# The first z loaded once and turned two neighbouring tiles at a time, with matmuls of zeros ahead and two first squares on ScalarE

## The chip, the core and the metric

The kernel runs on one NeuronCore of one Trainium2 chip. TensorE multiplies and transposes into PSUM, VectorE (DVE) and ScalarE (ACT) work on SBUF and PSUM, GpSimd (POOL) fills constants and issues indirect transfers, and SyncE (SP) issues most of the direct ones; ACT issues a few at the start. The metric is the device time of one execution in microseconds. The span of the profile is a little shorter than that time.

## The reference

Two blocks follow each other. The first is a gated attention over 8 batches of 2496 rows, the second sends each row to one of 8 experts by a hash of its token.

```python
scores = (1 / S) * z @ z.T              # z: (8, 2496, 64)
attn   = maximum(scores, 0) ** 2
x      = (u * (attn @ v)).reshape(B * S, 256)
for e in range(8):                      # rows with token_ids * 2654435761 % 8 == e
    out[mask] = maximum(x[mask] @ w1[e], 0) @ w2[e]     # 256 -> 1024 -> 256
```

Everything is in float32.

## The kernel before

A batch has T = 20 tiles of 128 rows; the last one, tile TM = 19, holds only R = 64 rows. Rows lie in the tiles so that partition p of tiles 0 to 18 holds 19 neighbouring rows of the batch; the 64 last rows are the short tile. Twenty tiles make NG = 5 groups of G = 4 tiles, and a batch is worked through group by group: the group's 512 columns are the queries, and all 20 tiles are the keys.

The order of all instructions is written out by hand (a manual schedule: each engine runs its instructions as the program lists them). It runs like this:

- **Loads.** `load_z(0)`, `load_v(0)`, `load_u(0, 0)` and `load_tokens()` are called first (lines 442 to 445). z of batch 0 is wanted with its 64 columns twice, side by side, so that one transpose of a [128 x 128] tile gives z transposed in partitions 0 to 63 and once more in partitions 64 to 127. So `load_z(0)` (lines 121 to 125) reads z from memory twice, once on SP's queue and once on ACT's, into a tile `[P, T, 2, K]`; its pieces in SBUF are 64 numbers, 256 bytes, long. `tiles_io` (lines 100 to 112) issues one transfer for tiles 0 to 18 and, with `twice=True`, two for the short tile, into partitions 0 to 63 and 64 to 127. v, u and the later batches' z follow on SP's queue; the token ids are on ACT's.
- **Turning.** `turn_z(0, g)` (lines 155 to 158) transposes the four tiles of a group on TensorE into one PSUM tile `z_ps`, and ScalarE copies it whole into `zT`. Later batches are turned on VectorE (line 153).
- **Scores.** `scores(b, g)` multiplies, for every tile t, the turned tile t with the turned group (line 181). Even t use partitions 0 to 63 of `zT`, odd t partitions 64 to 127; such a pair of 64-row matmuls runs on TensorE at the same time. The relu goes to ScalarE or VectorE in turn (lines 185 to 188) and the tile is noted in `to_square`.
- **Squares.** `square(n)` takes the n oldest tiles from that list. In batch 0 it works on VectorE (line 202), in the others on ScalarE (line 200). Ahead of the first group it is called with EARLY = 2 (line 474), after all 20 relus of the group are issued.
- **Attention.** `attend` (line 256) multiplies the squared tile with v into two accumulators, tile by tile; the squares of tiles two ahead, pieces of the routing (`places`, between lines 297 and 416, on VectorE mostly) and the indirect writes are put between. `gate` (line 265) multiplies with u, and `place_x` (line 433) writes the rows to `x_rows` in expert order.
- **Experts.** After the attention, blocks of 256 rows are read back and go through the two expert matmuls (lines 566 and 579), and the result is written by an indirect transfer (line 582). The first expert matmuls wait for the first rows read back.

PSUM buffers with the tag `mm` form one ring of six: the five `z_ps` tiles and the score tiles share it in the order of use. `zn`, the loaded z, has one buffer; the load of batch 1 into it waits until batch 0 is turned. `zero` is a [128 x 256] tile of zeros, filled by GpSimd (lines 281 and 282), from which SP later clears `x_rows` (line 288). `odd` is a [64 x 256] scratch tile for the last short group of a batch (line 236).

Of the kernel before, what the change touches and what calls it, by code (L numbers as in the profile page):

```python
# [10 lines left out]
F32 = mybir.dt.float32  # L11
# [13 lines left out]
def kernel(  # L25
# [10 lines left out]
    nc = tc.nc  # L36

    B, S, D = u.shape
    K = z.shape[-1]
    N = B * S  # L40
    E, _, F = moe_w1.shape
# [3 lines left out]
    P = 128  # L45
    TM = S // P
    SM = TM * P
    R = S - SM
    T = TM + 1
    assert R == 64 and K == 64  # L50
    G = 4
# [13 lines left out]
    def pool(name, bufs, **kw):  # L65
        return ctx.enter_context(tc.tile_pool(name=name, bufs=bufs, **kw))

    const = pool("const", 1)
    mm_ps = pool("mm_ps", 6, space=bass.MemoryType.PSUM)
    acc_ps = pool("acc_ps", 2, space=bass.MemoryType.PSUM)  # L70
    npool = pool("npool", 1)
# [12 lines left out]


    short = const.tile([P, T, R], F32)
    nc.gpsimd.memset(short[R:P, TM, :], 0.0)
    odd = const.tile([R, D], F32)
    ident = const.tile([P, P], F32)
    make_identity(nc, ident[:])  # L90

    def width(t):
        return P if t < TM else R

    def group(g):
        return range(g * G, min(T, g * G + G))

    def tiles_io(dram, b, tiles, sb, store, eng, twice=False):  # L100

        rows = dram[ds(b * S, S), :]
        whole = [t for t in tiles if t < TM]
        pairs = []
        if whole:
            n = len(whole)
            pairs.append((rows[0:SM, :].rearrange("(p t) d -> p t d", t=TM)[:, ds(whole[0], n), :], sb[:, 0:n, :]))
        if TM in tiles:
            for i in range(2 if twice else 1):
                pairs.append((rows[SM:S, :], sb[ds(i * R, R), len(whole), :]))  # L110
        for d, s in pairs:
            eng.dma_start(out=d if store else s, in_=s if store else d)

    uf, vf, zf = (x.rearrange("b s d -> (b s) d") for x in (u, v, z))
    zn, zT, v_sb, u_sb, x_sb, made, mirror, to_square, to_turn, gated = {}, {}, {}, {}, {}, {}, {}, [], [], []
# [3 lines left out]

    def load_z(b):  # L120
        if b == 0:
            zn[b] = npool.tile([P, T, 2, K], F32, name="zn")
            for i in range(2):
                tiles_io(zf, b, range(T), zn[b][:, :, i, :], False, nc.scalar if i else nc.sync, twice=True)
            return
        zn[b] = npool.tile([P, T, NQ, Q], F32, name="zn")
        rows = zf[ds(b * S, S), :]
        for q in range(NQ):
            cols = ts(q % 2, Q)
            o = zn[b][ts(q, Q)]  # L130
            for t, m in ((slice(0, TM), rows[0:SM, cols].rearrange("(j i t) k -> i t j k", i=Q, t=TM)),
                         (TM, rows[SM:S, cols].rearrange("(j i) k -> i j k", i=Q))):
                if t == TM:
                    for h in range(2):
                        nc.sync.dma_start(o[:, TM, ds(h * R // Q, R // Q), :], m)
                else:
                    nc.sync.dma_start(o[:, t], m)

    def load_v(b):
        v_sb[b] = vpool.tile([P, T, D], F32, name="v_sb")  # L140
        for g in range(NG):
            tiles_io(vf, b, group(g), v_sb[b][:, g * G:, :], False, nc.sync, twice=True)
# [5 lines left out]
    def turn_z(b, g):  # L148
        if g == 0:
            zT[b] = zpool.tile([P, T * P], F32, name="zT")  # L150
        o = zT[b][:, ts(g, G * P)]
        if b:
            nc.vector.transpose(o, zn[b][:, ts(g, G)].rearrange("p t j k -> p (t j k)"))
            return
        ps = mm_ps.tile([P, G * P], F32, name="z_ps", tag="mm")
        for i, t in enumerate(group(g)):
            nc.tensor.transpose(ps[:, ts(i, P)], zn[b][:, t].rearrange("p h k -> p (h k)"), ident[:])  # L157
        nc.scalar.copy(o, ps[:])

    def whole(g):  # L160

        return range(G if g < NG - 1 else G - 1)
# [5 lines left out]
    def mirrored(b):  # L168
        return b > 0

    def fresh(b, g):

        return range(g * G if mirrored(b) else 0, T)

    def scores(b, g):

        n = sum(width(t) for t in group(g))
        for t in fresh(b, g):
            h = ds(t % 2 * K, K)
            ps = mm_ps.tile([P, G * P], F32, name="s_ps", tag="mm")  # L180
            nc.tensor.matmul(ps[:, 0:n], zT[b][h, ts(t, P)], zT[b][h, ds(g * G * P, n)], start=True, stop=True)  # L181
            if t % G == 0:
                made[b, g, t // G] = apool.tile([P, G, G * P], F32, name="a", tag="a")
            a = made[b, g, t // G][:, t % G, 0:n]
            if t % 4 == 3 or t % 4 == 1 and not mirrored(b):
                nc.vector.tensor_scalar_max(a, ps[:, 0:n], 0.0)  # L186
            else:
                nc.scalar.activation(a, ps[:, 0:n], AF.Relu)  # L188
            to_square.append((b, g, t))

    def square(n):
        for b, g, t in to_square[:n]:
            a = made[b, g, t // G][:, t % G, :]
            m = len(whole(g)) * P
            pairs = [(a[:, 0:m], a[:, 0:m])]
            if m < G * P:
                pairs.append((short[0:width(t), t, :], a[0:width(t), ds(m, R)]))
            for o, x in pairs:
                if mirrored(b):
                    nc.scalar.square(o, x)  # L200
                else:
                    nc.vector.tensor_mul(o, x, x)  # L202
            if mirrored(b) and t // G > g and (t % G == G - 1):
                to_turn.extend((b, g, t // G, r, c) for r in range(NQ) for c in range(NQ))
        del to_square[:n]
# [72 lines left out]
    token = const.tile([P, B, T], I32)  # L278

    tok = const.tile([P, B, T, 2], I32)  # L280
    zero = const.tile([P, D], F32)
    nc.gpsimd.memset(zero[:], 0.0)
    CLEAR = T // 2
    assert NS % CLEAR == 0

# [144 lines left out]
    def place_x():  # L430
# [5 lines left out]
        tc.declare_no_dep(st.ins, group="x", reason="each token has its own slot")  # L436
        tc.add_to_no_dep_group("x", st.ins)

    order = tc.manual_schedule()
    order.__enter__()  # L440

    load_z(0)
    load_v(0)
    load_u(0, 0)
    load_tokens()
    for g in range(NG):
        turn_z(0, g)
# [3 lines left out]
    EARLY = 2  # L451
# [3 lines left out]
    i = 0  # L455
# [15 lines left out]

    mirror_pool = ExitStack()
    scores(0, 0)
    square(EARLY)
    for n, (b, g) in enumerate(groups):
        if n + 1 < len(groups):
            load_u(*groups[n + 1])
        if g == 0 and b + 1 < B:
            load_z(b + 1)
            load_v(b + 1)  # L480
# [5 lines left out]
        for k in range(2):  # L486
            for t in range(EARLY):
                attend(b, g, t, acc, [2 * k, 2 * k + 1])
            square(2)
            turn_scores(2)  # L490
            between()
        for t in range(EARLY, TM - LATE):
            if g == NG - 1 and b + 1 < B and t % 2 == 0 and t // 2 <= NG:
                turn_z(b + 1, t // 2 - 1)
            attend(b, g, t, acc, range(G))
            if t % G == G - 1 and (b, t // G, g) in mirror and g < NG - 1:
                mirrors.append(mirror.pop((b, t // G, g)))
            square(2)
            turn_scores(2 + (t % 3 == 0))
            between()  # L500
# [6 lines left out]
        if n + 1 < len(groups):  # L507

            while len({k[:3] for k in to_turn}) + len(fresh(*groups[n + 1])) // G > NG + (g + 1 < NG):
                turn_scores(1)  # L510
            scores(*groups[n + 1])
# [140 lines left out]
```

## Time and profile before

| what | value |
|---|---|
| median of three runs | 2717.02 us (2716.9 to 2718.02) |
| the profiled execution's own time | 2718.32 us |
| its span | 2716.4 us |
| TensorE, matmuls | 2681.2 us busy, 99% of the span |
| VectorE, ScalarE, GpSimd busy | 1190.3, 576.2, 478.7 us |
| granted TensorE clock, mean | 0.997 |
| first matmul (a transpose, line 157) starts at | 9.46 us |
| first attention matmul (line 256) starts at | 24.17 us |
| first expert matmul (line 566) waits for rows read back | 15.3 us |

The profile is read as follows. The page gives each engine's busy time, then the groups of instructions by line with the mean duration of one, and the idle time before them with what ended it. The chain of waits goes back from the last instruction to what released each step; its window on the first 60 us shows the start of the kernel. The timeline lists instructions in order of time. The table by windows gives each engine's busy time in a stretch, the granted clock and the transfer rate. The table of transfers gives the median time from issue to landing. All times are counted from the start of the span.

### The profile page before, as it was taken

Reading aid. Unit: us, or ns where it says so; the run is one execution under the profiler, and the core shown is the slowest. Engines: PE = TensorE matmul, PEld = TensorE weight load, DVE = VectorE, ACT = ScalarE, POOL = GpSimd, SP = SyncE. Lnnn points to the kernel's source line nnn. Section 1 sums busy time; section 2 is a strip of 40 time slices with the busy share of each in tenths; the row PEclk is TensorE's granted clock in tenths of the full one; section 3 lists DMA queues with packets and bytes.
Section 4 is the critical chain, followed back from the end, with each engine's and each line's share of the span. In section 5 each row is a group of like instructions: output and inputs, shape, how many; then the busy total and the mean of one; then the engine's idle time right before and its main releaser. Section 6 shows DMA issues by size and latency. Waiting matters only on the chain.

```text
span 2716.4 us, 32950 instructions
## 1 busy us (share of the span) xinstructions
PE 2681.2 (99%) x12650; PEld 2250.2 (83%) x12650; DVE 1190.3 (44%) x1875; ACT 576.2 (21%) x1151; POOL 478.7 (18%) x500
## 2 busy tenths in 40 slices
PE   8999999999999999999999979999999999999998
PEld 6777887888888887887878868888888888888887
DVE  5655956848838838758659411111111111111111
ACT  2013214214222233123132101111111111111111
POOL 0221222122212221222101111111111111111111
PEclk9999999999999999999999989999999999999999
DMA  9612113013103121031101077777777777777773
GB/s 283 212 31 73 32 31 88 16 32 88 31 23 82 31 50 60 26 89 32 32 15 31 23 191 189 188 188 188 194 190 193 191 189 191 190 189 188 189 186 104
DMA packets 334256, 308.84 MB, mean 114 GB/s; under 512 B 186732, under 2 KB 293117, under 8 KB 334096
## 3 DMA queue, kind: packets, MB, share of 16 engines
q1 hardware_dynamic: 309424, 264.78, 38.5%
q0 software_dynamic: 20496, 41.10, 5.0%
q8 instruction: 102, 1.67, 0.3%
q10 hardware_dynamic: 4176, 0.82, 0.2%
q14 instruction: 58, 0.48, 0.1%
HBM read 243.25 MB, written 64.13 MB: 113 GB/s over the span
## 4 chain that ended last, share of the span: by engine, by line
PE 55%; issue 37%; POOL 6%; DMA 2%; POOLq 0%; DVE 0%
PE acc L256 44%; PE s_ps L181 8%; POOL out_dram L582 5%; PE acc L250 1%; DMA out_dram<-o_sb,idx 1%; PE q_ps L231 1%; DMA zn<-in_z_dram 0%; POOLq L582 0%; POOL x_rows L433 0%; PE z_ps L157 0%; DVE upto L350 0%; DVE x_sb L265 0%; DVE a L202 0%; POOLq L647 0%; PE cnt_ps L345 0%
## 5 line engine op out<-in xcount | busy, mean ns | idle before, releaser
L256 PE MATMUL acc<-v_sb,a 128*128 128x256 f32 x3760 | 826.8, 380 | 2.5 <-DVE a L202 1.4
L256 PEld LDWEIGHTS acc<-v_sb,a 128*128 128x128 f32 x3760 | 711.0, 190 | 128.0 <-issue 29.0
L215 DVE STREAM_TRANSPOSE m<-a 32x512 f32<-32x512 f32 (+1 forms) x1120 | 757.2, 676 | 19.5 <-ACT a L200 2.7
L566 PE MATMUL h_ps<-zT,w 128*128 128x256 f32 x2592 | 587.2, 380 | 16.5 <-DMA zT<-x_rows 15.3
L579 PE MATMUL o_ps<-w,hT 128*128 128x256 f32 x2592 | 585.2, 379 | 0.0
L566 PEld LDWEIGHTS h_ps<-zT,w 128*128 128x128 f32 x2592 | 493.6, 191 | 84.6 <-issue 15.7
L579 PEld LDWEIGHTS o_ps<-w,hT 128*128 128x128 f32 x2592 | 492.5, 190 | 66.9
L574 DVE TENSOR_SCALAR hT<-h_ps 128x512 f32<-128x512 f32 x162 | 112.0, 691 | 951.4 <-PE h_ps L566 951.4
L256 PE MATMUL acc<-v_sb,m 128*128 128x256 f32 x2016 | 439.7, 379 | 0.0
L256 PEld LDWEIGHTS acc<-v_sb,m 128*128 128x128 f32 x2016 | 383.1, 190 | 52.0
L188 ACT ACTIVATE a<-s_ps 128x512 f32<-128x512 f32 (+1 forms) x365 | 193.6, 593 | 913.5 <-PE s_ps L181 905.0
L433 POOL DMA_INDIRECT x_rows<-x_sb,slot_i x160 | 157.8, 986 | 1089.8 <-DVE x_sb L265 917.1
L582 POOL DMA_INDIRECT out_dram<-o_sb,idx x162 | 157.5, 972 | 978.8 <-ACT o_sb L581 964.0
L181 PE MATMUL s_ps<-zT 64*128 64x512 f32 (+1 forms) x1040 | 230.4, 586 | 0.0
L186 DVE TENSOR_SCALAR a<-s_ps 128x512 f32<-128x512 f32 (+1 forms) x155 | 106.0, 684 | 283.1 <-PE s_ps L181 282.0
L200 ACT ACTIVATE a<-a 128x512 f32<-128x512 f32 (+1 forms) x420 | 221.5, 623 | 0.0
L581 ACT COPY o_sb<-o_ps 128x256 f32<-128x256 f32 x162 | 60.3, 372 | 743.7 <-PE o_ps L579 743.7
L181 PEld LDWEIGHTS s_ps<-zT 64*128 64x128 f32 x1040 | 116.8, 187 | 89.1 <-issue 61.5
L421 POOL DMA_INDIRECT slot_tokens<-token,addr x160 | 159.3, 996 | 161.2 <-DVE addr L415 110.9
L572 ACT ACTIVATE hT<-h_ps 128x512 f32<-128x512 f32 x162 | 96.7, 597 | 242.1 <-PE h_ps L566 242.1
L265 DVE SCALAR_TENSOR_TENSOR x_sb<-acc,u_sb 128x256 f32<-128x256 f32 x152 | 57.7, 419 | 58.4 <-PE acc L256 57.8
L238 DVE TENSOR_TENSOR odd<-odd,q_ps 64x256 f32<-64x256 f32 x8 | 3.3, 414 | 168.9 <-ACT odd L236 168.9
(67 smaller groups left out, 331.5 us busy)
## 6 DMA issues: line engine op xcount, KB each, us to landing
w<-in_moe_w_dram SPq DMA_DIRECT2D x324, 256.0 KB, 6.7
w<-in_moe_w_dram SPq DMA_DIRECT2D x81, 1024.0 KB, 6.1
x_rows<-zero SPq DMA_DIRECT2D x10, 2176.0 KB, 15.0
zT<-x_rows SPq DMA_DIRECT2D x324, 64.0 KB, 6.0
v_sb<-in_v_dram SPq DMA_DIRECT2D x32, 512.0 KB, 4.5
u_sb<-in_u_dram SPq DMA_DIRECT2D x32, 512.0 KB, 4.0
zn<-in_z_dram SPq DMA_DIRECT2D x28, 304.0 KB, 5.6
v_sb<-in_v_dram SPq DMA_DIRECT2D x8, 384.0 KB, 7.3
```

The source lines that it names most:

```text
L181: nc.tensor.matmul(ps[:, 0:n], zT[b][h, ts(t, P)], zT[b][h, ds(g * G * P, n)], start=True, stop=True)
L186: nc.vector.tensor_scalar_max(a, ps[:, 0:n], 0.0)
L188: nc.scalar.activation(a, ps[:, 0:n], AF.Relu)
L200: nc.scalar.square(o, x)
L215: nc.vector.transpose(mirror[b, a, g][ts(c, Q)].rearrange(squares)[:, 0:m, ts(r, Q)], made[b, a, g][ts(r, Q)].rearrange("p t (s q) -> p (t ...
L256: nc.tensor.matmul(acc[i // 2][:, i % 2, :], lhs(b, g, t, i), v_sb[b][:, t, :], start=(t == 0 and i % 2 == 0), stop=(t == TM - 1), skip_gr ...
L421: st = nc.gpsimd.indirect_dma_start(out=slot_dram[:, None], out_offset=bass.IndirectOffsetOnAxis(ap=addr[0:n, c:c + 1], axis=0), in_=token ...
L433: st = nc.gpsimd.indirect_dma_start(out=x_dram[:, :], out_offset=bass.IndirectOffsetOnAxis(ap=slot_i[0:width(c % T), c:c + 1], axis=0), in ...
L566: nc.tensor.matmul(ps[:, i, :], w1[j][:, c, ts(f + i, P)], xT[j][:, :, c, :], start=(c == 0), stop=(c == DP - 1))
L574: nc.vector.tensor_scalar_max(o, ps[:], 0.0)
L579: nc.tensor.matmul(ps[:], hT[j][:, f, ts(t, P)], w2[j][:, f, :], start=(f == 0), stop=(f == FP - 1))
L582: st = nc.gpsimd.indirect_dma_start(out=out[:], out_offset=bass.IndirectOffsetOnAxis(ap=idx[:, j * TB + t:j * TB + t + 1], axis=0), in_=o[ ...
```

## The change

Five things are edited.

- z of batch 0 is loaded once, into a tile `[P, T + 1, K]` from its second place on, on SP's queue alone. A partition's 19 rows are now one piece of 4864 bytes in memory and in SBUF. VectorE copies the short tile (place T) to place 0, so that tile T - 1 stands before tile 0.
- `turn_z(0, g)` transposes places t and t + 1 together. Of the result, partitions 64 to 127 hold the group's tiles and are copied by VectorE; partitions 0 to 63 hold the tiles one earlier and are copied by ScalarE to their own columns of `zT` (for group 0 in two pieces, as tile T - 1 belongs at the end).
- Five matmuls of zeros [128 x 128] by [128 x 256] are put ahead of everything on TensorE; their result isn't used. The tile `zero` is filled first on GpSimd for them.
- ScalarE copies one number from `zero` to `odd` ahead of its two transfers.
- The squares of tiles 0 and 1 of the first group are made on ScalarE, right after the relu of tile 10, and no more on VectorE after all relus.

In the built program each of ScalarE's copies of the turned z waits for VectorE's copy of the same group.

```diff
     short = const.tile([P, T, R], F32)
-    nc.gpsimd.memset(short[R:P, TM, :], 0.0)
     odd = const.tile([R, D], F32)
+    zero = const.tile([P, D], F32)
+    nc.gpsimd.memset(zero[:], 0.0)
     ident = const.tile([P, P], F32)
     make_identity(nc, ident[:])
+    nc.gpsimd.memset(short[R:P, TM, :], 0.0)
...
         if b == 0:
-            zn[b] = npool.tile([P, T, 2, K], F32, name="zn")
-            for i in range(2):
-                tiles_io(zf, b, range(T), zn[b][:, :, i, :], False, nc.scalar if i else nc.sync, twice=True)
+            zn[b] = npool.tile([P, T + 1, K], F32, name="zn")
+            tiles_io(zf, b, range(T), zn[b][:, 1:, :], False, nc.sync, twice=True)
+            nc.vector.tensor_copy(zn[b][:, 0, :], zn[b][:, T, :])
             return
...
         ps = mm_ps.tile([P, G * P], F32, name="z_ps", tag="mm")
         for i, t in enumerate(group(g)):
-            nc.tensor.transpose(ps[:, ts(i, P)], zn[b][:, t].rearrange("p h k -> p (h k)"), ident[:])
-        nc.scalar.copy(o, ps[:])
+            nc.tensor.transpose(ps[:, ts(i, P)], zn[b][:, t:t + 2].rearrange("p t k -> p (t k)"), ident[:])
+        nc.vector.tensor_copy(o[K:P], ps[K:P, :])
+        for i, n in ((0, G), ) if g else ((0, 1), (1, G - 1)):
+            nc.scalar.copy(zT[b][0:K, ds((g * G + i - 1) % T * P, n * P)], ps[0:K, ds(i * P, n * P)])
...
             to_square.append((b, g, t))
+            if (b, g, t) == (0, 0, T // 2):
+                square(EARLY, nc.scalar)
...
-    def square(n):
+    def square(n, eng=None):
...
-                if mirrored(b):
+                if mirrored(b) or eng is nc.scalar:
                     nc.scalar.square(o, x)
...
-    zero = const.tile([P, D], F32)
-    nc.gpsimd.memset(zero[:], 0.0)
...
+    WARM = 5
     order = tc.manual_schedule()
     order.__enter__()
+    nc.scalar.copy(odd[0:1, 0:1], zero[0:1, 0:1])
+    warm = mm_ps.tile([P, D], F32, name="warm", tag="mm")
+    for _ in range(WARM):
+        nc.tensor.matmul(warm[:], zero[:, 0:P], zero[:], start=True, stop=True)
     load_z(0)
...
     scores(0, 0)
-    square(EARLY)
```

## The prediction

> **What bounds the kernel now.** I read the page first. TensorE's matmuls fill nearly the whole span, so only time in which TensorE is idle or slow can be won, and only before the first attention matmul does the change touch anything.
>
> ```profile
> PE 2681.2 (99%) x12650; PEld 2250.2 (83%) x12650; DVE 1190.3 (44%) x1875; ACT 576.2 (21%) x1151; POOL 478.7 (18%) x500
> ```
>
> Of the 35.2 us without a matmul, 15.3 lie at the first expert matmul, which the change doesn't reach. Next I read the chain of waits over the first 60 us (start, duration, what).
>
> ```profile
> 0.82 8.50 DMA zn<-in_z_dram
> 9.32 0.14 issue
> 9.46 4.50 PE z_ps L157 x20
> 13.96 8.84 PE s_ps L181 x40
> 22.80 0.02 issue
> 22.83 0.69 DVE a L186
> 23.52 0.61 DVE a L202
> 24.13 0.04 issue
> 24.17 20.99 PE acc L256 x96
> ```
>
> This is the ground that can be won: 9.46 us until z lands, 4.5 us of transposes, about 8.6 us of scores (which stay), and 1.4 us in which TensorE waits for VectorE's last relu and first square. From 24.17 on the instruction lists of both kernels are the same on every engine, so I assume that everything later moves rigidly with that start.
>
> Third, the clock. The table by windows (stretch, length, busy times; the number after POOL is the granted clock) says 1.00 for the start, and shows the gate closing and opening only at the change to the experts. The weight loads (start, us) show it too.
>
> ```profile
> 9.46:14.00 4.54, 4.54 (x22) 4.21 (x22) 0.00 (x0) 3.02 (x6) 0.00 (x0) 1.00 1.02 333
> 1588.00:1590.00 2.00, 2.00 (x6) 1.58 (x5) 0.00 (x0) 0.00 (x0) 0.00 (x0) 0.50 0.40 122
> 1590.00:1592.00 2.00, 2.00 (x9) 1.67 (x8) 0.00 (x0) 0.60 (x1) 0.00 (x0) 0.77 1.09 238
> 1592.00:1594.00 2.00, 2.00 (x11) 1.77 (x10) 1.18 (x2) 0.00 (x0) 0.00 (x0) 1.00 0.97 201
> ```
> ```profile
> 1588.32 0.34 PEld L566 LDWEIGHTS h_ps<-zT,w 128*128 128x128 f32 x1
> 1588.74 0.34 PEld L566 LDWEIGHTS h_ps<-zT,w 128*128 128x128 f32 x1
> 1591.97 0.19 PEld L566 LDWEIGHTS h_ps<-zT,w 128*128 128x128 f32 x1
> ```
>
> I do not believe the 1.00 at the start. At half clock the records of 256 columns start 0.427 us apart (1588.32, 1588.74, 1589.17), which is 1.667 ns a column; at full clock 152 of them take 33.00 us, which is 0.216 us or 0.844 ns a column. The transposes are records of 128 columns. ScalarE's copies of four of them start at 10.58, 11.44, 12.29, 13.14 and 14.00, so one transpose takes 3.42/16 = 0.2138 us, 1.670 ns a column: the half clock. The score pairs after them come every 0.858 us from the first one on, the full clock. So the gate opened at about 13.96, and the profile drew no event since none came before. The changes of the clock fit a free-running grid: down at 1577.25, up at 1590.91, down at 2713.81, that is 4 and 329 steps of 3.413 us; counted back, a step falls at 13.9 to 14.1. Against this stands that a weight load of the transposes takes 0.231 us, neither of the two durations above.
>
> **The rule against the row.** The Trainium skill ("TensorE: Matmul & The Clock Gate", Part 1) says that half rate is the default and that one busy window of about 3.4 us releases it; that agrees with the columns and not with the 1.00. Its Part 4 says that transposes do not count as busy for the gate. The trace speaks against that: only transposes stood between 9.46 and 13.89, and the scores ran at full rate at once. By Part 4 they would have run some 3.4 us longer at half rate. I follow the trace. By the printed 1.00 the zeros are worth nothing, and transposes stay at 4.3 us (rival 1).
>
> **The change, part by part.**
>
> *One load in long pieces.* Nearest rows, in the steady attention (transfers, KB each, median us to landing):
>
> ```profile
> u_sb<-in_u_dram SPq DMA_DIRECT2D x25, 512.0 KB, 4.0
> u_sb<-in_u_dram SPq DMA_DIRECT2D x6, 384.0 KB, 3.6
> zn<-in_z_dram SPq DMA_DIRECT2D x40, 8.0 KB, 3.4
> ```
>
> 128 KB more cost 0.4 us, so 608 KB take 4.0 + 0.75 x 0.4 = 4.3 us. The first issue of the kernel takes 0.70 us where a u load takes 0.33, so I add 0.37: 0.82 + 4.3 + 0.37 = 5.5. The two short transfers are issued behind it at 1.52 and about 2.13 (0.6 us each); 2.13 + 3.4 = 5.55, and they follow the long one through the same queue. The tokens, now behind a table load and the one-number copy on ACT, are issued at about 2.4 and share the engines: their small pieces filled 7.4 to about 9.7 before, so the cost is between 0 and 2.3 us. I take 0.1, as the long transfer is nearly through when they start.
>
> *The copy of the short tile* queues first on VectorE, with the group copies behind it; TensorE's first transpose waits for it. Nearest rows 0.16 (128x7) and 0.24 us (128x160): 0.19, with two hops of about 0.07. Transposes can start at 5.55 + 0.1 + 0.33 = 6.0 by z.
>
> *The zeros.* Their tile is filled 0.3 us after 0.82; the first matmul starts at about 1.5. Five matmuls are ten records of 256 columns: 4.3 us at half clock, ending at 5.8; 2.2 us at full clock, ending at 3.7. Both hide under the load of z; if z came at once they would cost up to 4.3. With TensorE busy from 1.5, a wholly busy step of the grid ends between 4.9 and 8.3, wherever the grid lies; a step busy for a third (7.13 to 10.55 before) did not open it. Mean 6.6.
>
> *Transposes and their copies.* A transpose takes 0.214 at half clock, 0.108 at full. The copies are now split, VectorE first and ScalarE behind it, group by group. VectorE: about 0.67 a group (the row of 128x480 from PSUM has 0.658); ScalarE: 0.59 (0.587 for 128x512). The first score reads tile 3 in the lower half, which comes with group 1 of ScalarE's copies. With the gate open from the start, group 0 stands in PSUM 0.7 after the first transpose, VectorE ends groups 0 and 1 at 1.43 and 2.1, ScalarE group 1 at about 2.8: scores at 2.9. With the gate opening at 8.3, about 3.5. I take 3.2: scores start at 9.2, where they started at 13.89. Bounds 2.9 and 4.5. The later copies (VectorE until about 4.1, ScalarE until 4.8 after the first transpose) delay the first relus by up to 0.4 us, which the ring of six PSUM buffers covers.
>
> *Squares on ScalarE.* Two of 0.63 us are put between relus that leave ScalarE 0.26 us a pair. The relu of tile 12 ends at 7.9 after the first score instead of about 6.9; tile 18 takes its buffer at 7.72: a stall of about 0.3. The later group without a wait needs 8.78 us from first score to first attention matmul (54.25 to 63.03); so 8.78 + 0.27 = 9.05. Bounds: 8.8, and 10.3 (as before). Both squares are done by then; those of tiles 2 and 3 follow on VectorE until about 11.1 after the first score, where 12.5 is early enough.
>
> *At no cost.* The table load (1.28 us) moves from 8.84 to the very start, under the z load; uncovered it would add its length. ACT's three z issues go. On SP's queue v and u come earlier: 3.6 MB at the 400 GB/s seen at 12 to 13 us are through by about 14, v's first group is wanted at 18. The load of z for batch 1 waits for the turning and, new, for VectorE's copy; behind it stand v of batch 1, the clearing and u, all wanted 20 us later or more. The reordered fills on GpSimd are done by 4.5, as before.
>
> *Sum.* 6.0 + 3.2 + 9.05 = 18.25 against 24.17: 5.9 us less. In the profiled execution the gate opened early in its possible stretch (12.9 to 16.3 for a start at 9.46); an average run loses 0.3 more, so I take 6.1. The profiled execution, 2716.4 of span and 1.9 around it, would fall from 2718.3 to 2712.2; from the median, 1.3 below it, I forecast 2717.0 - 6.1 = 2710.9.
>
> **Rivals.**
> 1. *The clock was full all along.* For it: the printed 1.00 and the odd weight load. Against: the columns. Transposes stay at 0.214, scores start at 6.0 + 4.43, the attention at 19.5: 4.7 us, 2712.3.
> 2. *z lands later than I think*, the short rows sitting among the tokens' pieces. First transpose at up to 8.3, scores 2.9 later, attention at about 20.2: 4 us, 2713.0. For it: the same engines serve both queues. Against: the long piece is nearly through.
> 3. *More is won:* no stall in the scores, gate open early and tails quick (transposes at 5.6): 5.6 + 2.9 + 8.8 = 17.3, 6.9 us, with the average grid 7.2: 2709.8.
> 4. *Slower:* the 4864-byte pieces are spread over few of the 16 transfer engines. At 400 GB/s the z load moves for 1.6 us; with four engines 6.2. From a first transpose at about 10.7 on, after which the gate has closed again (TensorE idle for a whole step) and the scores come 4.4 later, the change loses: on two engines the data take 12.4 us, and the start is later by some 6 us: 2723. Against it: v's pieces of 4096 bytes in the same form run at 400.
>
> **How the numbers follow.** My forecast has 0.55, rival 1 0.18, rival 2 0.10, rival 3 0.14, the slower one 0.03. The range is 2709.0 to 2713.1: rivals 1 to 3, with half a microsecond or so for the spread of runs (1.1 us before). A measurement of this kernel can tell about 0.2%, 5.4 us, from no change. My forecast is beyond it in about 9 of 10 of its share, rival 3 always, rivals 1 and 2 hardly: 0.67 faster, 0.30 within, 0.03 slower.
>
> **What would show it.** Right: first transpose at 5.7 to 6.3, transposes starting 0.108 apart for most of the twenty, the first score near 9.2, the first attention matmul near 18.2 with no wait for VectorE. Wrong: transposes at 0.214 throughout (rival 1); a first transpose past 7 with z as releaser (2); gaps over 0.5 us between score pairs after tile 12; or a later stage that gives the gain back, first of all another wait than 15.3 us at the first expert matmul.

## The result, and the profile after

The changed kernel takes 2714.16 us in the median of 20 runs (2712.78 to 2716.26 but for one disturbed run of 8578.93; 2713.93 without it), the kernel before 2718.18 in as many: a ratio of 0.9985 with a 95% interval of 0.9978 to 0.9992. That is 4.0 us less, where 6.1 were forecast, and the time lies above the forecast range (2709.0 to 2713.1). The gain is clear of no change by its interval, but it is 0.15%, where the prediction gave a chance of 0.67 to more than 0.2%.

The profiled execution looks quite otherwise. It took 2712.78 us with a span of 2710.5, where 2712.2 was forecast for it, and its attention starts close to the forecast. First the engines' row of the page and the group of first expert matmuls:

```profile
PE 2683.1 (99%) x12660; PEld 2252.3 (83%) x12660; DVE 1192.7 (44%) x1879; ACT 577.1 (21%) x1155; POOL 479.5 (18%) x500
...
L578 PE MATMUL h_ps<-zT,w 128*128 128x256 f32 x2592 | 587.1, 380 | 16.4 <-DMA zT<-x_rows 15.0
```

Nothing is given back later: the wait at the experts is 15.0 us (15.3 before). The chain of waits over the first 60 us, as before (start, us, what):

```profile
1.90 4.54 DMA zn<-in_z_dram
...
6.54 0.20 DVE zn L127
...
6.84 0.64 PE z_ps L162 x4
...
7.50 0.71 DVE zT L163
...
8.23 1.20 ACT zT L165 x3
...
9.47 8.96 PE s_ps L188 x40
18.43 20.92 PE acc L265 x96
```

The attention starts at 18.43, against 24.17 before and 18.25 forecast. No wait for VectorE is left in front of it. But z came at 6.45, not at 5.55, and the chain runs from z through the two rows of copies, not through TensorE: the turning is so fast that its evictions bound it. The zeros' weight loads show why (timeline of TensorE's weight loads):

```profile
3.90 0.34 PEld L454 LDWEIGHTS warm<-zero 128*128 128x128 f32 x1
4.33 0.20 PEld L454 LDWEIGHTS warm<-zero 128*128 128x128 f32 x1
```

At 4.33 a weight load falls from 0.34 to 0.20 us: the gate opens there, while the granted clock of the views says 1.00 from the start. The trace holds the same instant as its first clock event (4.33); before its first event it has nothing to draw. So in this one run all transposes ran at full clock. The question is then why the median of twenty runs is 1.4 us above this run, when the profiled run of the kernel before (2718.32) is at its median (2718.18).

Two theories stood against each other. **A:** the gate's grid of 3.413 us (the steps at whose ends the clock can change) falls differently in each run, and since z comes later than reckoned, TensorE is idle between the zeros and the turning; where that gap spoils the step, the gate opens only during the turning or the scores. **B:** the clock has no part in it; z's landing or something later varies.

### The profile page after: what moved, and what is told of

It is laid out like the page before. It is cut to its first block, busy times and chain, and to the rows that moved or that the text cites. A ratio compares the mean times of both kernels' runs of the same rounds, so it can differ in the third digit from the quotient of the medians.

```text
span 2710.5 us, 32975 instructions
## 1 busy us (share of the span) xinstructions
PE 2683.1 (99%) x12660; PEld 2252.3 (83%) x12660; DVE 1192.7 (44%) x1879; ACT 577.1 (21%) x1155; POOL 479.5 (18%) x500
## 4 chain that ended last, share of the span: by engine, by line
PE 55%; issue 37%; POOL 6%; DMA 2%; POOLq 0%; DVE 0%; ACT 0%; SPq 0%; DVEq 0%
PE acc L265 44%; PE s_ps L188 8%; POOL out_dram L594 5%; DMA out_dram<-o_sb,idx 1%; PE acc L259 1%; PE q_ps L240 1%; POOL x_rows L440 0%; POOLq L594 0%; DMA zn<-in_z_dram 0%; DVE upto L357 0%; DVE x_sb L274 0%; POOLq L659 0%; DVE a L211 0%; ACT zT L165 0%; PE cnt_ps L352 0%
## 5 line engine op out<-in xcount | busy, mean ns | idle before, releaser
L578 PEld LDWEIGHTS h_ps<-zT,w 128*128 128x128 f32 x2592 | 493.5, 190 | 84.6 <-issue 15.3
```

The costliest lines, as they stand in the source:

```text
L578: nc.tensor.matmul(ps[:, i, :], w1[j][:, c, ts(f + i, P)], xT[j][:, :, c, :], start=(c == 0), stop=(c == DP - 1))
```

## The experiments

All kernels compute the whole reference. Each was timed side by side with the kernel before, three or four kernels to a series; "before" is its median in that series. The ratios are made of all runs of a series, not of the medians, and can differ a little from the quotient of these.

**The changed kernel again, and eight zeros, and none.** The first run has no edit. The other two:

```diff
-    WARM = 5
+    WARM = 8
```
```diff
-    warm = mm_ps.tile([P, D], F32, name="warm", tag="mm")
-    for _ in range(WARM):
-        nc.tensor.matmul(warm[:], zero[:, 0:P], zero[:], start=True, stop=True)
```

> The changed kernel once more, unchanged. In its first profile the attention started at 18.36, the weight loads of the zeros show the clock opening at 4.33, and the time was 2712.8, while the median of twenty runs is 2714.2. Theory A (the gate's free-running grid falls differently in every run; where no step of 3.41 us is busy enough between the start of the zeros at 1.2 and the turning, the gate opens only during turning or scores): transposes of 0.21 us or score pairs of 1.7 us show in this profile or not, by chance; time 2712.8 if the gate opened before the turning, up to 2716 if after; spread of the runs some 3 us. Theory B (the clock is no matter, the spread comes from the landing of z or from transfers later on): transposes are 0.108 in every profile, and z's landing or the wait of the first expert matmul differs by the same as the time.

> Eight matmuls of zeros in place of five, so that TensorE is busy until z is there (16 records: 6.8 us at half clock, about 5 with the gate opening in between, from 1.2 on). Theory A: there is a wholly busy step in every run, the gate opens before or just as the turning starts, and the runs draw together near the fast end of the changed kernel: median 2712.5 to 2713.3, 1 us or more below the changed kernel's median. Theory B: same median as the changed kernel, 2714, or up to 1 us more where the zeros end after z is there.

> No matmuls of zeros at all; all else as in the changed kernel. Theory A: transposes start at 6.8 at half clock, 0.214 us each, first score about 4.4 later at 11.3 and the gate opens between 10.2 and 13.7, partly in the scores: attention starts at 20.3 to 21.2, and the time is 2 to 3 us above the changed kernel's fast end, 2715 to 2716. Theory B: as the changed kernel, 2714, with the transposes at 0.108.

Before took 2717.91 us. The changed kernel took 2713.20 (2712.69 to 2715.97; ratio 0.9985, 0.9976 to 0.9994), with eight zeros 2713.20 (2712.51 to 2714.26; 0.9983, 0.9974 to 0.9992), with none 2715.33 (2714.58 to 2716.53; 0.9990, 0.9981 to 0.9999).

The changed kernel's 30 runs of both series, without that of 8578.93, seem to fall in two heaps: 17 from 2712.7 to 2713.9 and 13 from 2714.4 to 2716.3. The line between them is drawn by eye: the gap is 0.5 us wide, and one of 0.9 us parts the three highest runs from the rest. With eight zeros no run is above 2714.26 and the standard deviation is 0.55 us against 1.09. Its median did not come 1 us below the changed kernel's in the same series, as A had it; the changed kernel happened to have 7 of 11 runs in the low heap there. The means differ by 0.4. So the spread speaks for A, the median alone decides nothing. Without zeros the chain reads:

```profile
7.07 4.50 PE z_ps L162 x20
11.57 9.03 PE s_ps L188 x40
20.60 20.92 PE acc L265 x96
```

The transposes take 4.50 us in place of 2.4, the first score comes 2.1 us later than in the changed kernel and the attention at 20.60, inside what A expected; B, which wanted transposes at 0.108 us, is out. The zeros are worth about 2 us here (2.1 by medians, 1.6 by means).

**The first two squares back on VectorE.**

```diff
-            if (b, g, t) == (0, 0, T // 2):
-                square(EARLY, nc.scalar)
...
     scores(0, 0)
+    square(EARLY)
```

> The first two squares back on VectorE, after all relus, all else as in the changed kernel. If the squares on ScalarE are worth what the prediction says (a wait of 1.42 us taken away, 0.3 put in its place), the attention starts 1.1 us later after the first score (10.1 against 9.0) and the median is 1.1 us above the changed kernel's in the same call. If the wait is hidden now, no difference.

Measured: 2715.07 us (2713.76 to 2715.46; 0.9988, 0.9979 to 0.9997). From first score to attention it takes 10.20 us against 8.96, 1.24 more, where 1.1 was expected; by means it is 1.1 us slower than the changed kernel, by medians 1.9. But this profile showed more, since the gate opened late in it. Its chain ("issue" is idle time to which the view gives no releaser; here TensorE is out of zeros and z isn't there):

```profile
1.18 4.63 PE warm L452 x10
5.81 1.10 issue
6.91 3.88 PE z_ps L162 x20
10.79 8.83 PE s_ps L188 x40
...
20.34 0.61 DVE a L209
...
20.99 20.99 PE acc L263 x96
```

And the groups of the turning by form, in the window from 6 to 11 us, first of the changed kernel, then of this one (count, busy, mean ns, idle before):

```profile
L162 PE MATMUL z_ps<-ident,zn 128*128 128x128 f32 x20 | 2.4, 274 | 1.7 <-DVE zn L127 1.7
```
```profile
L162 PE MATMUL z_ps<-ident,zn 128*128 128x128 f32 x20 | 3.9, 380 | 1.1 <-issue 1.1
```

The same five zeros and the same load, but the transposes take 3.9 us in place of 2.4 and the first score is 1.3 us later. The gate opened at 10.00 by the trace's event, and there the transposes change from 0.213 to 0.109 us from start to start. The step before ran from 3.18 to 6.59; TensorE ended the zeros at 5.81 and turned from 6.91 on, so by its records that step was busy for 2.63 of its 3.41 us, 77%, and that did not open the gate. In the changed kernel's first profile the step up to 4.33 was busy from 1.18 on, 92%, and did. This is theory A in one pair of profiles: the same start up to the scores, two outcomes.

**Why z is late: the tokens.** The forecast let the tokens be issued behind ACT's table load and copy, at 2.4. The timeline of the changed kernel shows it otherwise (the copy is written first in the program):

```profile
1.17 0.43 ACTq L301 DMA_DIRECT2D tok<-in_moe_token_ids_dram  x1
...
2.11 0.19 ACT L451 COPY odd<-zero 1x1 f32<-1x1 f32 x1
```

The issue came 0.94 us ahead of the copy and while the table load (0.81 to 2.09) still ran. Between 4 and 5 us the queues then moved (packets, MB, share of 16 engines):

```profile
q10 hardware_dynamic: 1326, 0.15, 104.3%
q1 hardware_dynamic: 121, 0.07, 24.0%
```

1326 packets of tokens on ACT's queue (q10) fill the engines just when z's short rows are due on SP's (q1). The test: tokens later on ACT, behind the copies of z, with five and with six zeros; and tokens on SP's queue behind v and u, with five and with six.

```diff
-    load_tokens()
     for g in range(NG):
         turn_z(0, g)
+    load_tokens()
```
```diff
-        nc.scalar.dma_start(tok[...
+        nc.sync.dma_start(tok[...
```

> The changed kernel with the two token transfers issued on ScalarE's queue after the copies of the turned z, not ahead of them. In the changed kernel 1436 small pieces moved between 4 and 5 us, just when z's short rows were due, and the first transpose started at 6.84 to 6.94 in place of the predicted 6.0. If the tokens hold the short rows: first transpose at 5.7 to 6.1, TensorE's gap after the five zeros shrinks to half a microsecond or less, the gate opens before or at the turning in nearly every run, and the median is 0.8 to 1.5 us below the changed kernel's 2713.2 to 2714.2. If the short rows' own transfers take that long: first transpose stays near 6.9, and the time stays.

> Tokens late as in the run before, and six matmuls of zeros, so that no gap is left at half clock (1.2 to 6.3). Theory A (gate's grid, idle gap): first score always near 8.8 to 9.2, no run with transposes at 0.214 beyond the first few, the narrowest spread of all and the lowest median, near 2712.2. Theory B: the same as the run before, or slower by up to 0.4 where the sixth holds the turning.

Measured, with 2718.61 before: five zeros 2712.93 (2712.16 to 2713.84; 0.9981, 0.9972 to 0.9990), six 2713.50 (2712.03 to 2714.54; 0.9983, 0.9974 to 0.9992). The first transpose came at 6.40 with five, later than the 5.7 to 6.1 that I expected, though earlier than 6.84; no token moved before it, so what held it there is open. With six the zeros themselves held it until 6.5. The six did not give the lowest median or the narrowest spread, against A's expectation: they leave no gap, and their runs still spread over 2.5 us. So the gap is not the only thing that moves the time by that much. The scores grew to 9.33 us, which I put down to the two issues that now stood between ScalarE's copies and its first relus. That was tested:

> The changed kernel with the two token transfers issued on SP's queue, behind v and the first u. With the tokens late on ScalarE's queue the first transpose came at 6.4, but the scores took 9.3 in place of 8.95, because the two issues held up ScalarE's first relus. If that is the cause: first transpose at 6.0 to 6.4, scores in 8.9 to 9.0, attention at about 17.6 to 18.0 where the gate opens early, median 2712.2 to 2712.7. If the longer scores have another cause: attention at 18.3 again and a median like that run's, 2712.9.

> As the run before, with six matmuls of zeros. In the grid theory five leave a gap of half a microsecond or less before the turning at 6.0 to 6.4 and open the gate in most runs, six in all; but where the gate opens only after 6.3, the sixth holds the turning by 0.1 to 0.4. Expected: median within 0.3 of the run with five, spread no wider. Slower by more than 0.5 would mean that the zeros are now in z's way.

Measured, with 2718.01 before: 2712.38 (2711.71 to 2713.33; 0.9978, 0.9969 to 0.9987) with five and 2712.25 (2711.82 to 2714.11; 0.9978, 0.9968 to 0.9987) with six. The chain with five zeros:

```profile
1.18 4.63 PE warm L454 x10
5.82 0.23 issue
6.04 0.64 PE z_ps L162 x4
...
8.68 8.96 PE s_ps L188 x40
17.63 20.92 PE acc L265 x96
```

The transposes start at 6.04, the time forecast for the changed kernel; the gap is 0.23 us; the scores are back at 8.96; the attention starts at 17.63. The median is 5.6 us below before, and the standard deviation, 0.42 us, is the smallest of all kernels. With six zeros it is 0.65, wider and not "no wider", through one run: the profiled one, 2714.11, where the nine others end at 2712.41. So the tokens delay z, and the delay makes the gap; that the gap makes the second heap is likely, but not shown (see below the table of profiles). Ten of the eleven runs with five zeros lie at 2712.73 or below, as one of the changed kernel's 30 does; the two were not timed side by side, and the intervals of their ratios overlap.

**Parts alone on the kernel before.** The load and the turning alone are the changed kernel without the zeros (as above) and with the squares on VectorE (as above). The squares alone put the two edits of `square` and `scores` on the kernel before. The zeros alone put twelve matmuls there, to last until z lands, and fill their tile earlier, as in the change:

```diff
+    warm = mm_ps.tile([P, D], F32, name="warm", tag="mm")
+    for _ in range(12):
+        nc.tensor.matmul(warm[:], zero[:, 0:P], zero[:], start=True, stop=True)
```

> The changed kernel without the zeros and with the first squares on VectorE: only the single load and the turning in pairs are left of the change. First transpose near 6.9 to 7.1 against 9.46 before, transposes at half clock as before, first score 4.4 to 4.5 later (11.5), the wait for VectorE's square back (1.4): attention at about 21.7, 2.4 us earlier than before; time 2.0 to 2.6 below the kernel before. The time outside the span (1.9 before, 2.3 with the change) is 2.3 if it belongs to the load and the turning.

> The kernel before with nothing but the first two squares on ScalarE after the relu of tile 10. If this part is additive: the wait of 1.42 us at the first attention matmul is gone, a stall of 0.2 to 0.4 stands in the scores, attention 1.1 to 1.25 us earlier (22.9 to 23.1), time 1.1 to 1.3 below the kernel before; time outside the span as before, 1.9.

> The kernel before with nothing but twelve matmuls of zeros ahead (24 records from 1.2 on, ending between 8.1 and 9.7, so no whole step of the grid is idle before z lands at 9.3). Grid theory: transposes at 0.108 in place of 0.214 and scores at full rate from the first pair in every run, attention at 21.7 to 22.0 in place of 24.2 and later; median 2.0 to 2.6 below the kernel before, spread narrower. If the clock had been full all along: no gain, or a loss of up to 0.3.

> The kernel before once more, for a second profile of it. Grid theory: the transposes take 4.5 us again or less at their end, and where the grid falls later than 13.9 some score pairs come 1.7 us apart; attention starts anywhere from 23.6 to 25.4, and the rest of the kernel, attention to the last copy, takes 2685.5 within 0.6 as in all profiles so far. Time within 0.3 of the median of the kernel before; time outside the span 1.9.

| kernel | median | before | ratio (95%) |
|---|---|---|---|
| load and turning alone | 2715.87 | 2718.61 | 0.9994 (0.9985 to 1.0003) |
| squares alone | 2717.20 | 2718.61 | 0.9997 (0.9988 to 1.0006) |
| twelve zeros alone | 2716.32 | 2718.01 | 0.9992 (0.9983 to 1.0001) |
| before again | 2717.72 | 2718.01 | 0.9998 (0.9989 to 1.0007) |

None of the three parts is clear of no change by its interval alone; the profiles say more. With the load alone the transposes start at 6.77 and, the gate opening at 10.19 in that run, take 4.03 us; the attention starts at 21.01, 0.7 earlier than I expected for a later grid. Its runs spread from 2714.6 to 2720.5, for which no profile shows the reason. With the squares alone the chain has

```profile
13.74 9.50 PE s_ps L181 x40
23.24 20.92 PE acc L258 x96
```

and the wait for VectorE is gone. The scores take 9.50 us, since in this run the gate opened only at 15.15, within them; so the attention starts 0.1 to 0.3 later than expected. With the zeros alone:

```profile
9.32 2.38 PE z_ps L159 x20
11.69 8.83 PE s_ps L183 x40
```

the transposes take 2.38 in place of 4.50, on the kernel before; the attention starts at 21.90, as expected. The median is 1.7 us lower, a little less than the 2.0 that A asked for. In the second profile of the kernel before the gate opened at 14.82, within the scores, which took 9.21 us in place of 8.84. All profiles side by side (us; "opened" is the trace's first clock event, "rest" is from the attention's start to the start of the last ScalarE copy, "half clock" is how long TensorE then runs at half clock at the first expert matmuls):

| kernel | opened | first transpose | first score | attention | rest | half clock |
|---|---|---|---|---|---|---|
| before | 13.94 | 9.46 | 13.96 | 24.17 | 2685.6 | 3.6 |
| before again | 14.82 | 9.60 | 14.10 | 24.67 | 2685.6 | 4.3 |
| changed | 4.33 | 6.84 | 9.47 | 18.43 | 2685.4 | 3.5 |
| changed again | 5.44 | 6.94 | 9.58 | 18.53 | 2685.5 | 4.7 |
| eight zeros | 5.63 | 6.92 | 9.54 | 18.49 | 2685.6 | 5.0 |
| no zeros | 12.04 | 7.07 | 11.57 | 20.60 | 2685.8 | 5.8 |
| squares on VectorE | 10.00 | 6.91 | 10.79 | 20.99 | 2685.1 | 3.0 |
| tokens late, five zeros | 6.32 | 6.40 | 9.03 | 18.36 | 2686.2 | 5.4 |
| tokens late, six zeros | 6.91 | 6.47 | 9.29 | 18.63 | 2684.4 | 2.8 |
| load and turning alone | 10.19 | 6.77 | 10.80 | 21.01 | 2685.2 | 3.5 |
| squares alone | 15.15 | 9.25 | 13.74 | 23.24 | 2686.5 | 6.0 |
| zeros alone | 5.58 | 9.32 | 11.69 | 21.90 | 2686.1 | 3.8 |
| tokens on SP, five zeros | 5.75 | 6.04 | 8.68 | 17.63 | 2686.1 | 5.8 |
| tokens on SP, six zeros | 7.09 | 6.46 | 9.38 | 18.34 | 2686.8 | 5.7 |

**A rival for the second heap.** The rest is not the same everywhere: it spreads over 2.4 us. Two things account for it to within 0.3 us: the first expert matmul starts 1562.4 to 1563.6 us after the attention, and from there TensorE runs at half clock for 2.8 to 6.0 us, of which half is lost, until the gate opens a second time. The granted clock (the third number from the end) shows that opening at 1584.70 in the changed kernel's first profile, where the matmuls start at 1581.18, and at 1587.46 in the last kernel of the table, where they start at 1581.74:

```profile
1584.50:1585.00 0.50, 0.50 (x4) 0.39 (x3) 0.00 (x0) 0.08 (x1) 0.00 (x0) 0.80 0.99 229
```
```profile
1586.00:1588.00 2.00, 2.00 (x7) 1.59 (x7) 0.00 (x0) 0.13 (x1) 0.00 (x0) 0.63 1.04 231
```

These are 3.5 and 5.7 us at half clock, and the difference is 1.1 us of work. The last profile is that of the run of 2714.11: its gate opened at 7.09, after three transposes, its first score came at 9.38, and it is still 1.7 us above the highest of the other nine. So a run can lie high though the gate opened before most of the turning, and the changed kernel's second heap may hold such runs too; neither of its own two profiles is of the second heap.

## Why the prediction was wrong

The mechanism held where z was there in time; one condition, two sizes and the base were wrong.

- **The clock.** The argument from nanoseconds a column against the printed 1.00 was right. Transposes behind an opening of the gate run at the full rate in all profiles, and the odd weight load of 0.231 us is what a transpose's weight load takes at half clock: at full clock it is 0.141. Rival 1 is out. What the Trainium skill says in "TensorE: Matmul & The Clock Gate", Part 4, that transposes don't count as busy, doesn't hold for these float32 transposes: with the load alone, the step from 6.77 to 10.19 held nothing but transposes, and the gate opened at its end.
- **The step that failed** is this one: "With TensorE busy from 1.5, a wholly busy step of the grid ends between 4.9 and 8.3, wherever the grid lies." It supposed that TensorE goes from the zeros (5.8) straight to the turning (6.0). It doesn't: the turning starts at 6.8 to 6.9, the gap is 1.1 to 1.7 us, and a step that holds it may not open the gate. With the squares on VectorE, which has the same start, 77% of a step was not enough, the transposes took 3.9 us in place of 2.4 and the first score came 1.3 us later. In the two profiles of the changed kernel itself the gate opened in time. What late openings cost its median is inferred: 13 of 30 runs lie in the higher heap, whose median is 1.8 us above the lower one's, and that is 0.8 us of the mean; it is less if some of the 13 are high for the rest of the kernel.
- **z's landing.** This made the gap. First transpose at 6.84 to 6.94 where 6.0 was forecast, and at 6.04 with the tokens on SP's queue, so the 0.1 us taken for the tokens was about 0.9; with the tokens late on ScalarE it came at 6.40, so that up to 0.4 of it may be z's own spread. The bounds given (0 to 2.3) held it; the value was near the wrong end, since I let the issue wait behind the table load, until 2.4, and it came at 1.17. Where the gate opens early this costs little, as the copies took 2.6 us from first transpose to first score where 3.2 were forecast for a mean grid.
- **Rival 2** named this cause, the short rows among the tokens' pieces, and a gain of 4 us. That the measured gain is 4.0 is luck: it put the attention at 20.2, and the profile has 18.43.
- **Squares.** 8.96 us from first score to attention where 9.05 was forecast, and 10.2 without: right.
- **Time outside the span.** The prediction left it at 1.9 us; it is 2.2 to 2.3 in all runs of the changed kernel. With the load and turning alone it is 2.2 to 2.4 in seven runs of eleven and 1.9 in four, with the squares alone and with the zeros alone 1.9 to 2.0 in all. So it comes with the load and the turning, though not in every run. Why, no run shows.
- **The base.** The forecast of 2710.9 stood on a median of three runs, 2717.0; over twenty it is 2718.2. That is 1.2 of the 3.3 us by which the absolute forecast missed. The other 2.1 are the gain, 4.0 in place of 6.1. The profiled pair gains 5.5 (2718.32 to 2712.78), with 0.2 of the shortfall at the attention's start and 0.4 outside the span; the medians gain 1.5 less than that. How this 1.5 is shared among late openings, the second opening and the draw of the runs (in the second series the gain was 4.7) no run separates.
- **Two slips in the sums.** The last change of the clock is at 2713.89, not 2713.81; the 329 steps of 3.413 us stand. And the 0.3 for an average grid was taken off the profiled execution too, to which it doesn't belong: 5.9 less would have been 2712.4.
- **Nothing was given back later.** The rest of the kernel kept its length, as assumed, but for the first rows' arrival at the experts and the second opening of the gate, 2.4 us between the extremes of all profiles.

## What to carry to other kernels

Whether matmuls of zeros ahead of the first work open the clock in time depends on where the grid falls, if a gap stands between them and the work: size them to the arrival of the data, and take more than one profile, since one shows one position of the grid. With the same five zeros the gate opened at 4.33, ahead of a gap of 1.7 us, in one profile, and not before the turning in another with a gap of 1.1 us. A clock row that says full from the start may only mean that no event came before; the time per column tells. When a first load is made faster, look what else is issued in the same microsecond: here the tokens' small pieces on another queue held two small transfers by 0.4 to 0.9 us.

## What the runs showed of the hardware that was not expected

- How full a step of the grid must be, over the fourteen profiles and both openings in each ("busy" by the trace's records): none that was busy for 77% or less opened the gate (77%: the one up to 6.59 with the squares on VectorE; 76%: squares alone, up to 1588.70), and every one from 83% up did (83%: tokens late, six zeros, at 1583.87; 85%: tokens late, five zeros, at 6.32). In between, nothing was measured.
- An open gate was closed by steps that were busy for 41% (squares alone, at 2711.68) and less, and by none of 42% (tokens on SP, five zeros, up to 2705.69) and more.
- A transfer on ScalarE's queue was issued at 1.17, while the table load ran until 2.09 and a copy written ahead of it ran from 2.11 to 2.30.
- The float32 transpose of [128 x 128] takes 0.213 us from start to start at half clock and 0.109 at full; twenty of them take 4.50 and 2.38 us.
